# Sliding-window attention whose second half is cut by query chunk instead of by head group, with more staging buffers and earlier loads

## The chip, the cores and the metric

The kernel runs on one core of one Trainium2 chip. The metric is device time in microseconds (us) of a whole execution, the median of several runs. A separate execution, taken by the profiler, gives the rows quoted below. The engines are PE (TensorE, matmuls; PEld its weight loads), DVE (VectorE), ACT (ScalarE), POOL (GpSimd) and SP (SyncE, which issues most DMAs).

## What is computed

Two layers run on 2048 positions of width 576 and their outputs stand side by side. Layer A is attention with 32 heads of 18, where a query sees itself and the 255 positions before it; layer B is a long convolution whose filter comes from a state-space model.

```python
def A(x, wqkv, wo):                      # 32 heads, Dh = 18, window W = 256
    q, k, v = split(x @ wqkv)
    scores = q @ k.T * Dh ** -0.5
    mask = (i - j >= 0) & (i - j < W)
    p = softmax(where(mask, scores, -1e9))
    return concat_heads(p @ v) @ wo
def B(u, A, B, C, log_dt, Dskip):
    dt = exp(log_dt)
    K = real(einsum("dn,dnl,dn->dl", C, exp(dt * A * l), dt * B))
    return irfft(rfft(pad(u)) * rfft(pad(K)))[:L] + u * Dskip
return concatenate([A(...), B(...)], -1)
```

## The kernel before

**Stages.** `front` loads and scales the weights. Then the projection to q, k and v (`proj`, stored to the DRAM buffers `qd` and `vd`), the filter's tables (`tables`) and the first transform stage of the input (`s1_u`) are interleaved. Then attention begins, and everything that is left runs inside it.

**Filter's first stage.** `s1_k` has 16 parts. Each does 8 matmuls (line 521), copies the results to two staging tiles `g1` of the pool `s1k` (line 145 on ScalarE, every fourth on VectorE, line 147) and stores them to `gk` over SP (line 523). The pool has 4 buffers. Two parts run ahead of attention, seven more before the first scores, seven in items 0 to 6.

**Units and items.** Heads come in eight groups `g` of four. Attention's work is cut into 16 units: units 0 to 7 are groups 0 to 7 for queries 0 to 1023 (the first half, `hf` = 0), units 8 to 15 the same groups for queries 1024 to 2047. A unit has two chunks `c` of 512 queries, a chunk three banks `b`: 96 items. In loop step `n` of `attention` the scores of item `n` are emitted together with the values of item `n - 2`, some steps of the maxima for a later unit, and parts of the convolution and of the output projection. `merge` takes the next step of the stream that is furthest behind its share; the instructions of each engine run in the order in which they are emitted. `self.after(1, ...)` puts a DMA at the beginning of the next item.

**One unit.** `load_unit(i + 2)` is called at the first item of unit `i` and loads Q and K over SP (lines 681, 682) into one of three sets, and V over GpSimd's queue (line 685) into one of four V buffers. `gmax` copies Q into a block-diagonal form `qb` (line 693), multiplies 32 blocks of 32 queries by their 288 keys (line 702, PSUM pool `ring` of 3 banks), and VectorE takes the maximum of each with a bias mask (line 709); the result goes into a row of Q by DMA. It starts at the fourth item of the unit two before. `scores` multiplies K and Q (line 743, PSUM pool `stp`), ScalarE takes the exponential (line 745), GpSimd clears the triangles at the window's edges (line 754). `values` accumulates in PSUM (line 766); ScalarE copies out (line 774).

**Normalization.** `norm`, for units 0 to 13, moves the denominators by small DMAs over SP (line 810), spreads their reciprocals by a transpose (line 817), multiplies (825), splits into two float16 parts (826, 828) and stores them to `od` over GpSimd's queue (line 832, four DMAs). `norm_chunk`, for units 14 and 15, does it for 512 queries with two transposes on VectorE (lines 781 to 794) without SP. Group 7 is not stored: it stays in SBUF (`h7`).

**Output projection.** The output's rows are four chunks of 512, a chunk 8 pieces (4 row tiles by 2 column halves). A whole piece has 15 matmuls (line 978): three products for each of four blocks `k` of 126 rows of `od`, and three for group 7. `wo_operands` loads the blocks from `od` over SP (line 966). Chunks 0 and 1 (`wo_first`) run in items 62 to 85. Chunks 2 and 3 need the second half of all groups, so `wo_part` does k = 0, 1 of both (16 pieces of 6 matmuls, items 87 to 96, results kept in SBUF), and `wo_rest` the other 9 matmuls of each piece and the addition on VectorE (line 1012): for half of chunk 2 at item 97, for the others behind all else.

**Convolution.** `conv` starts at item 10. In its last stage (from about item 78) 16 steps each load a tile of the spectra `h` over SP (line 615) and of the input over GpSimd's queue (line 619), two steps ahead; VectorE multiplies the input by Dskip (line 633, one step ahead), PE transforms (line 637), VectorE adds into `y`, which has two buffers (line 640), and SP stores (`self.after`, line 134).

**Attention's start.** `attention_start` loads unit 0, then the identity and the bias mask (`att_consts`), then unit 1; then `gmax(0)` is merged with `s1_k`.

## Time and profile before

| | us |
|---|---|
| runs: median of 3 (lowest, highest) | 1009.77 (1008.87, 1018.71) |
| profiled execution | 1002.49 |
| its span, first to last instruction | 1000.8 |
| PE, DVE, POOL, ACT busy | 833.7, 684.2, 598.9, 560.9 |
| first scores begin | 445.8 |
| last value matmuls end | 977.3 |

A busy time is a sum over instructions; matmuls are pipelined, so a busy PE is not PE at its peak. In the answers by stretches each row has the stretch, its length, then for each engine the busy us and in brackets the number of instructions, the granted clock of TensorE as a share of its full clock, the mean share of the time that the 16 DMA engines were busy, and GB/s. In a row in order of time stand start, duration, engine, line, operation, output, input, shape, count, and in square brackets the engine's idle time before it and what ended it. In a row of groups stand busy time, mean ns, idle time before and what ended it. In a row of waits stand the total, the number of times and, for one engine's list, the longest.

### The profile page before, as it was taken

How to read it: one execution, taken by the hardware profiler on the slowest of the kernel's cores; microseconds unless marked ns; L12 is line 12 of the kernel's file. 1: busy time of each engine (PE TensorE's matmuls, PEld its weight loads, DVE VectorE, ACT ScalarE, POOL GpSimd, SP SyncE). 2: the span in 40 equal slices, each digit the busy share in tenths (PEclk: the TensorE clock that was granted, in tenths of full speed). 3: DMA queues.
4: the chain of work that ended last, by engine and by line, in shares of the span. 5: the costliest groups of instructions: out<-in, count | busy, mean ns of one | idle time of the engine just before them, and what ended most of it. 6: DMA issues, size and time to landing. Idle time of an engine off the chain costs nothing.

```text
span 1000.8 us, 26986 instructions
## 1 busy us (share of the span) xinstructions
PE 833.7 (83%) x10364; PEld 443.5 (44%) x10364; DVE 684.2 (68%) x1815; ACT 560.9 (56%) x901; POOL 598.9 (60%) x733
## 2 busy tenths in 40 slices
PE   0287989888999999689988888788888999988687
PEld 0034645464566557444433333333333444444345
DVE  5689477467574576357678778888777666668464
ACT  1455766566766775235655565565655555545460
POOL 2118567485686677602476867577866775666680
PEclk9998999999999999989899999999999999999899
DMA  8824535434543532634475675754658573687863
GB/s 304 257 71 123 141 106 123 100 83 114 129 105 76 134 94 76 220 126 148 131 161 149 172 184 166 177 151 124 145 153 202 139 182 104 168 213 232 225 175 128
DMA packets 139240, 150.35 MB, mean 150 GB/s; under 512 B 37464, under 2 KB 106248, under 8 KB 138344
## 3 DMA queue, kind: packets, MB, share of 16 engines
q1 hardware_dynamic: 131144, 131.75, 49.1%
q0 software_dynamic: 6512, 15.04, 5.6%
q10 hardware_dynamic: 1456, 1.84, 0.6%
q8 instruction: 82, 1.34, 0.6%
q14 instruction: 46, 0.38, 0.1%
HBM read 86.30 MB, written 61.01 MB: 147 GB/s over the span
## 4 chain that ended last, share of the span: by engine, by line
PE 24%; DVE 12%; issue 6%; DMA 4%; ACT 3%; POOL 3%; SPq 1%; DVEq 0%; ACTq 0%; POOLq 0%
PE po L766 5%; PE r L702 4%; PE r L978 4%; PE r L570 3%; PE r L562 3%; PE ST L743 2%; DVE jk L709 2%; ACT P L745 2%; DVE qb L693 2%; DVE osb L825 2%; DMA ol<-od 1%; POOL P L754 1%; DVE t L592 1%; DVE t L594 1%; PE r L637 1%
## 5 line engine op out<-in xcount | busy, mean ns | idle before, releaser
L709 DVE CUSTOM_DVE_ANT_0 jk<-r,bias 128x288 f32<-128x288 f32 (+7 forms) x512 | 199.8, 433 | 86.4 <-PE r L702 84.8
L754 POOL TENSOR_SCALAR_AFFINE_SELECT P<-P 128x512 f32<-128x512 f32 x240 | 168.9, 732 | 142.8 <-ACT P L745 140.2
L745 ACT ACTIVATE P<-ST,esc 128x1024 f32<-128x1024 f32 (+1 forms) x192 | 202.0, 1059 | 93.1 <-PE ST L743 92.6
L442 POOL TENSOR_TENSOR m<-A,tr 128x1024 f32<-128x1024 f32 x72 | 143.5, 2015 | 79.6 <-PE kp L480 79.5
L702 PE MATMUL r<-K,qb 128*64 128x288 f16 (+7 forms) x1024 | 130.6, 296 | 40.0 <-DVE qb L693 11.8
L702 PEld LDWEIGHTS <-qb 128*64 128x64 f16 x1024 | 58.4, 109 | 125.7 <-issue 72.9
L766 PE MATMUL po<-P,V 128*32 128x256 f32 (+2 forms) x1408 | 100.3, 397 | 11.9 <-ACT osb L774 3.9
L599 POOL TENSOR_TENSOR Y<-t,t 64x288 f32<-64x288 f32 x64 | 55.1, 861 | 63.3 <-DVE t L594 61.3
L480 PE MATMUL kp<-Q,m 128*32 128x64 f32 x4608 | 81.1, 223 | 11.3 <-issue 3.4
L480 PEld LDWEIGHTS kp<-Q,m 128*32 128x32 f32 x4608 | 70.1, 111 | 38.7 <-issue 24.4
L743 PE MATMUL ST<-Q,K 64*128 64x384 f16 (+2 forms) x704 | 73.6, 282 | 1.3 <-DMA Q<-mt 1.3
L420 POOL TENSOR_TENSOR tr<-tr,mab 128x768 f32<-128x768 f32 x18 | 33.9, 1884 | 43.6 <-ACT tr L389 43.6
L180 PE MATMUL pp<-xh,wh 128*128 128x512 f16 x180 | 51.0, 404 | 9.5 <-ACT xh L211 8.9
L766 PEld LDWEIGHTS po<-P,V 128*32 128x32 f32 x1408 | 36.2, 110 | 46.9 <-issue 28.7
L383 DVE TENSOR_TENSOR k<-x,k 128x512 f32<-128x512 f32 (+1 forms) x54 | 34.0, 641 | 33.5 <-ACT k L382 33.1
L180 PEld LDWEIGHTS <-wh 128*128 128x128 f16 x324 | 31.9, 100 | 53.8 <-issue 21.3
L600 POOL TENSOR_TENSOR Y<-t,t 64x288 f32<-64x288 f32 x64 | 52.0, 813 | 3.8
L180 PE MATMUL pp<-xh,wl 128*128 128x512 f16 x180 | 48.3, 394 | 0.0
L384 DVE TENSOR_SCALAR ab<-k 128x512 int32<-128x512 int32 (+1 forms) x54 | 47.8, 897 | 0.4
L342 DVE SCALAR_TENSOR_TENSOR qst<-pp,qst 128x512 f16<-128x512 f32 x36 | 24.7, 685 | 30.9 <-ACT qst L341 23.0
L145 ACT ACTIVATE g<-pp 128x288 f32<-128x288 f32 x75 | 29.1, 414 | 29.9 <-PE pp L521 19.1
L521 PE MATMUL pp<-ut,w 128*128 128x288 f32 x128 | 39.8, 433 | 6.6 <-DVE qst L342 5.2
(175 smaller groups left out, 1716.2 us busy)
## 6 DMA issues: line engine op xcount, KB each, us to landing
qd<-qst SPq DMA_DIRECT2D x72, 128.0 KB
gx<-g SPq DMA_DIRECT2D x32, 288.0 KB
gk<-g SPq DMA_DIRECT2D x32, 288.0 KB
tx<-gx SPq DMA_DIRECT2D x32, 288.0 KB
tk<-gk SPq DMA_DIRECT2D x32, 288.0 KB
h<-ho SPq DMA_DIRECT2D x16, 576.0 KB
Q<-qd SPq DMA_DIRECT2D x32, 216.0 KB
raw<-in_x_dram SPq DMA_DIRECT2D x16, 320.0 KB
```

What stands on the lines that cost most here:

```text
L180: self.nc.tensor.matmul(ps, u, v, start=(i == 0), stop=(i == len(ops) - 1))
L384: nc.vector.tensor_scalar(ab.bitcast(I32), k, 0x7FFFFFFF, None, op0=OP.bitwise_and)
L442: self.nc.gpsimd.tensor_tensor(m, A[:, ch, a0:a0 + 8].unsqueeze(3).to_broadcast(sh), tr[:, ch, part, 0:8].unsqueeze(2).to_broadcast(sh), o ...
L480: nc.tensor.matmul(kp[32 * st:32 * st + 32, c % 2 * JJ2 + j, :], m[:, ch, a0:a0 + 32], Q[:, ch, term % 2, :], start=(term == 0), stop=(ter ...
L599: nc.gpsimd.tensor_tensor(Y[par][0:64], t1[sl, 0], t2[sl, 0], op=OP.subtract)
L600: nc.gpsimd.tensor_tensor(Y[par][64:128], t1[sl, 1], t2[sl, 1], op=OP.add)
L702: nc.tensor.matmul(ps[64 * b:64 * b + 64, :n], self.qb[:, b, t, :], d["K"][:, b, k0:k0 + n], start=True, stop=True, skip_group_check=True)
L709: nc.vector.tensor_tensor_reduce(out=jk[:, :n], in0=ps[:, :n], in1=self.bias[:, 288 - n:], scale=1.0, scalar=-3e38, op0=OP.add, op1=OP.max ...
L743: nc.tensor.matmul(ps[:, u, o:o + n], d["K"][h, jp, k0:k0 + 128], d["Q"][h, jp, q0:q0 + n], start=True, stop=True, skip_group_check=True)
L745: nc.scalar.activation(pt[:, 2 * jp:2 * jp + 2, lo:hi], ps[:, :, lo:hi], AF.Exp, scale=self.esc)
L754: nc.gpsimd.affine_select(v, v, pattern=[[0, 4], [sg, 128]], compare_op=OP.is_ge, fill=0.0, base=-1 if far else 0, channel_multiplier=-sg)
L766: nc.tensor.matmul(self.po[32 * j:32 * j + 32, t0 * 128:t1 * 128], V[:, kb * 76 + 19 * j:kb * 76 + 19 * j + 32], pt[:, j, o:o + (t1 - t0) ...
```

## The change

Unit `i` of the second half, `i = 8 + 4c + g'`, is now groups 2g' and 2g' + 1 for the single chunk of 512 queries at 1024 + 512c. `runs(i)` gives its two runs, each with its own 768 keys, so K's tile grows from 1280 to 1536 columns and V's from 10 to 12 blocks of 76 (`key0` gives a chunk's first key block). Loads and stores of these units are two of half the queries in place of one. All groups of output chunk 2 come from units 8 to 11. Its projection is whole pieces (`wo_whole(2, 3)`) in items 84 to 96; `wo_part` does k = 0, 1 of chunk 3 alone, and `wo_rest` keeps seven PSUM banks (four of `stp`, three of `ring`) for chunk 3: k = 2 of seven pieces, k = 3, then group 7 and the addition piece by piece. Chunks 0 and 1 run in items 58 to 79. `norm` is used to unit 11 and `norm_chunk` from unit 12; unit 15's runs without pauses and stores group 6 over SP, after which block k = 3 of chunk 3 is loaded.

Besides: the pool `s1k` has 8 buffers in place of 4, and two parts of `s1_k` move from ahead of the first scores to items 7 and 8; at attention's start the order is unit 0, query copies, bias mask, identity, eight steps of `gmax(0)` with two parts of `s1_k`, unit 1, the rest; V is loaded three items after Q and K, into three buffers in place of four; the maxima's unused output `jk` is one fixed tile in place of one of a pool; and the convolution's last stage loads three steps ahead in place of two.

```diff
-HK = HQ + 256
+HK = HQ + 512
...
-        nx = [loadh(0), loadh(1)]
+        nx = [loadh(0), loadh(1), loadh(2)]
...
-            if qd < 14:
-                nx.append(loadh(qd + 2))
+            if qd < 13:
+                nx.append(loadh(qd + 3))
...
+    def runs(self, i):
+        if i < 8:
+            return [(i, 0, 0, HQ, 0, 256, HQ)]
+        c, g = divmod(i - 8, 4)
+        q0 = HQ + 512 * c
+        return [(2 * g + e, q0, 512 * e, 512, q0 - 256, 768 * e, 768) for e in range(2)]
+    def key0(self, i, c):
+        return 4 * c if i < 8 else 6 * c
...
+        for g, q0, qc, qn, k0, kc, kn in self.runs(i):
+            for u in range(2):
+                nc.sync.dma_start(d["Q"][64 * u:64 * u + 54, :, qc:qc + qn], heads(216 * g, q0, qn)[u])
+                nc.sync.dma_start(d["K"][64 * u:64 * u + 54, :, kc:kc + kn], heads(32 * 54 + 18 + 216 * g, k0, kn)[u])
+    def load_v(self, i):
+        V = self.V[i] = self.p["v"].tile([128, 12 * 76 + 16], F32, name="V")
+        for g, q0, qc, qn, k0, kc, kn in self.runs(i):
...
+            nc.gpsimd.dma_start(V[:, e - n:e].rearrange("p (t e) -> p t e", e=76),
+                                self.vd[g][:, k0 // 128:(k0 + kn) // 128])
...
-                jk = self.p["m"].tile([128, 288], F32, name="jk")
+                jk = self.jk
...
-                k0, q0 = (4 * c + r) * 128, (4 * c + t0) * 128
+                k0, q0 = (self.key0(i, c) + r) * 128, (4 * c + t0) * 128
...
+        g, q0 = self.runs(i)[c][:2]
+        for j in range(4 if g < 7 else 0):
+            f0 = 72 * g + 18 * j
+            (nc.gpsimd if i < 15 else nc.sync).dma_start(
+                self.od[:, f0:f0 + 18, q0:q0 + 512].rearrange("a p n -> p a n"), h[32 * j:32 * j + 18])
...
+                if k == 3 and i < 14:
+                    self.load_v(i + 2)
...
-            if n < 7:
+            if n < 9:
                 streams.append((part(s1k, 1), 1))
...
-            if n in (59, 67):
-                self.wo_operands((n - 59) // 8, 0, 4)
-            if 62 <= n < 86:
-                k = share(n - 62, 16, 24)
+            if n in (56, 64):
+                self.wo_operands((n - 56) // 8, 0, 4)
+            if n == 82:
+                self.wo_operands(2, 0, 4)
+            if n in (90, 96):
+                self.wo_operands(3, *((0, 2) if n == 90 else (2, 3)))
+            if 58 <= n < 80:
+                k = share(n - 58, 16, 22)
                 streams.append((part(wo0, k), k))
...
-            if n in (84, 88):
-                self.wo_operands(2 + (n - 84) // 4, 0, 2)
-            if n in (94, 96):
-                self.wo_operands(2 + (n - 94) // 2, 2, 4)
-            if 87 <= n < 97:
-                k = share(n - 87, 16, 10)
+            if 84 <= n < 97:
+                k = share(n - 84, 8, 13)
+                streams.append((part(wo2, k), k))
+            if 91 <= n < 97:
+                k = share(n - 91, 8, 6)
                 streams.append((part(wo1, k), k))
-            if n == 97:
-                streams.append((part(wo2, 4), 4))
...
-            if n >= 2 and n < 86 and (n - 2) % 6 == 5:
+            if n >= 2 and n < 74 and (n - 2) % 6 == 5:
                 norms.append(self.norm(items[n - 2][0]))
...
+        self.wo_operands(3, 3, 4)
...
-        for g in (wo1, wo2, self.wo_rest(3)):
-            for _ in g:
-                pass
+        self.wo_rest()
...
+    def wo_rest(self):
+        nc = self.nc
+        pss = []
+        for t in range(2):
+            ps = self.p["stp"].tile([128, 2, 512], F32, name="ST")
+            pss += [ps[:, 0, :288], ps[:, 1, :288]]
+        pss += [self.wo_ring() for n in range(3)]
+        for k in (2, 3):
+            for n in range(7):
+                self.wo_mm(pss[n], 3, n // 2, n % 2, k, k + 1, k == 2, False)
+        for n in range(8):
+            t, h = n // 2, n % 2
+            if n < 7:
+                ps = self.wo_mm(pss[n], 3, t, h, 4, 4, False, True)
+            else:
+                ps = self.wo_mm(self.wo_ring(), 3, t, h, 2, 4, True, True)
+            if h == 0:
+                y = self.p["wo2"].tile([128, D], F32, name="ya")
+            nc.vector.scalar_tensor_tensor(y[:, h * 288:h * 288 + 288], ps, self.osc, self.acc[n],
+                                           op0=OP.mult, op1=OP.add)
...
-            self.pool(ek, "s1k", 4, side="right")
+            self.pool(ek, "s1k", 8, side="right")
...
-            for n, b, s in (("att", 1, None), ("m", 2, None), ("v", 4, None), ("ring", 3, PSUM)):
+            for n, b, s in (("att", 1, None), ("m", 2, None), ("v", 3, None), ("ring", 3, PSUM)):
...
-                for _ in part(s1k, 1):
-                    pass
-                merge((self.gmax(0), 19), (part(s1k, 5), 5))
+                gm = self.gmax(0)
+                next(gm)
+                self.att_consts()
+                merge((part(gm, 8), 8), (part(s1k, 2), 2))
+                self.load_unit(1)
+                self.load_v(1)
+                merge((gm, 10), (part(s1k, 2), 2))
```

143 lines of the change are left out of this document (69 added, 74 removed).

## The prediction

> **What bounds the kernel now.** I read the page first, then the busy time by stretches, then who waits for whom, and last the rows in order of time at the two ends of attention.
>
> ```profile
> span 1000.8 us, 26986 instructions
> PE 833.7 (83%) x10364; PEld 443.5 (44%) x10364; DVE 684.2 (68%) x1815; ACT 560.9 (56%) x901; POOL 598.9 (60%) x733
> core 0: us, PE busy (x) PEld busy (x) DVE busy (x) ACT busy (x) POOL busy (x), PEclk, DMA share, GB/s
> 415.00:420.00 5.00, 2.38 (x15) 1.38 (x11) 1.60 (x13) 0.00 (x0) 0.99 (x3) 1.00 0.83 231
> 420.00:425.00 5.00, 0.73 (x2) 0.50 (x2) 0.00 (x0) 0.93 (x3) 0.00 (x0) 0.71 0.92 339
> 425.00:430.00 5.00, 4.92 (x22) 2.46 (x21) 3.37 (x17) 0.52 (x2) 0.00 (x0) 0.50 0.36 135
> 430.00:435.00 5.00, 4.31 (x22) 2.12 (x20) 2.46 (x12) 0.91 (x3) 0.00 (x0) 0.76 0.31 118
> 870.00:977.30 107.30, 88.34 (x854) 42.71 (x853) 69.29 (x184) 55.70 (x72) 75.86 (x128) 0.95 0.78 213
> 880.00:890.00 10.00, 6.33 (x60) 2.39 (x60) 6.28 (x21) 3.87 (x5) 5.23 (x9) 0.83 0.65 184
> 940.00:950.00 10.00, 4.51 (x20) 1.65 (x21) 3.48 (x7) 2.93 (x5) 3.23 (x7) 0.72 0.95 249
> 977.30:1000.80 23.50, 17.99 (x148) 13.86 (x144) 10.97 (x21) 1.23 (x2) 0.00 (x0) 0.96 0.34 121
> ```
>
> No engine is full for the whole span; TensorE comes nearest at 83%. Three places have slack that the change touches. At 415 to 425 us TensorE works 3.1 of 10 us and every engine is nearly still, while the DMA share is 0.83 and 0.92: attention's start waits for transfers. From 870 to 977.3 TensorE is busy 88.3 of 107.3 us, with holes at 880 to 890 (3.7 us idle) and 940 to 950 (5.5 us idle). From 977.3, the end of the last value matmuls, 23.5 us follow in which only the output projection runs.
>
> The profiled run took 1002.49 us, 1.7 us more than its span and 7.3 us below the median of the three runs, 1009.77 us. I add differences in us to the median, since nothing says where the runs differ.
>
> **Start of attention: minus 4.3 us.**
>
> ```profile
> 410.90 0.46 DVE L147 COPY g<-pp 128x288 f32<-128x288 f32 x1 [1.48 <-PE pp L521]
> 413.22 1.44 DVE L693 COPY qb<-Q 54x2048 f16<-54x2048 f16 x2
> 412.27 0.94 SPq L667 DMA_DIRECT2D bias<-in_c_bias_dram  x2
> 415.27 0.19 DVE L709 CUSTOM_DVE_ANT_0 jk<-r,bias 128x32 f32<-128x32 f32 x1
> 423.81 0.71 ACT L145 ACTIVATE g<-pp 128x288 f32<-128x288 f32 x2 [9.05 <-DMA gk<-g]
> 433.29 0.45 DVE L709 CUSTOM_DVE_ANT_0 jk<-r,bias 128x288 f32<-128x288 f32 x1
> 433.66 0.45 DVE L709 CUSTOM_DVE_ANT_0 jk<-r,bias 128x288 f32<-128x288 f32 x1
> 440.06 2.21 PE L521 MATMUL pp<-K,w 128*128 128x288 f32 x8
> 445.82 0.33 PE L743 MATMUL ST<-Q,K 64*128 64x384 f16 x1 [1.05 <-DMA Q<-mt]
> ```
>
> ScalarE waits 9.05 us for a store of the staging tile g, because the pool has 4 buffers (two parts of the filter's first stage) and unit 1's loads stand ahead of the stores. With 8 buffers four parts fit, and unit 1's loads come after the fourth: this wait goes. What is late next is the bias, whose clearing on VectorE and load on SP now stand behind the query copies. These follow the second part's copy, which ends at 411.36, and take 1.44 us: 412.8. Two issues (0.94 us) and a landing (from 413.21 to 415.27 at most, 2.06 us) put the first maximum at about 416, 0.7 us later than now. Behind the bias on SP stand the stores of parts 3 and 4; the eight buffers cover them. VectorE needs 0.37 us per maximum (433.29 to 433.66); with the exchange with TensorE I estimate half as much again, 1.1 us per pair, and 17.6 us for 16 pairs. Of seven parts that still run before the first scores two are done by 412.8; four of the rest, at 2.21 us and partly under VectorE, add 7 us. That ends near 438, against 445.82 for the first scores: 7.8 us. The two parts moved to items 7 and 8 (4.4 us of TensorE) come back at 0.8 of their length, 3.5 us; where the factor comes from is said below. Bounds: 0 if the bias or unit 1's late loads take the whole gain, 8 if the moved parts are hidden.
>
> The clock went to 0.50 and 0.76 in the ten microseconds after the hole, so 2.5 + 1.2 = 3.7 us of clock are lost there, which the 7.8 us hold. The Trainium skill (TensorE: Matmul & The Clock Gate, part 1 on the warmup) puts the way back to full clock at about 3.4 us of steady work at half rate, a loss of 1.7 us; as an estimate by that page the start would gain 2 us less. The trace shows the longer penalty, and I keep it.
>
> **Projection moved into attention: plus 7.2 us.**
>
> ```profile
> 741.35 0.59 ACT L774 ACTIVATE osb<-po 128x512 f32<-128x512 f32 x1
> 773.54 0.59 ACT L774 ACTIVATE osb<-po 128x512 f32<-128x512 f32 x1
> 812.34 0.59 ACT L774 ACTIVATE osb<-po 128x512 f32<-128x512 f32 x1
> 977.33 4.54 PE r L978 x36
> 986.66 10.13 PE r L978 x81
> ```
>
> A projection matmul costs 10.13 / 81 = 0.125 us. Chunk 2 now has its 8 pieces of 15 matmuls in items 84 to 96 (15.0 us) and loses 8 partial pieces of 6 (6.0 us): 9.0 us more TensorE work before the last values. How much of it shows? The copies at 741.35, 773.54 and 812.34 end units 8, 9 and 10, six items apart: 32.2 us without projection, then 38.8 us with 4 pieces (60 matmuls, 7.5 us). So 6.6 of 7.5 us showed there, 0.88; the last third has more holes than that stretch, and I take 0.8. 9.0 x 0.8 = 7.2 us. Starting chunks 0 and 1 four items earlier only moves work inside the same stretch. Bounds: 1 us (all in holes) and 9.
>
> **Prefetch of three instead of two: minus 8 us.**
>
> ```profile
> DVE X L633 <- DMA X<-in_u_dram: 9.6, 3, 4.2
> DVE t L633 <- DMA t<-in_u_dram: 8.3, 3, 4.3
> DVE t L640 <- DMA out_dram<-t: 5.6, 3, 2.0
> PE r L637 <- DMA tx<-h: 4.7, 1, 4.7
> ```
>
> In the convolution's last stage VectorE, working in order, stands 17.9 us for the input rows, TensorE 4.7 us for the spectra; gmax and scores stand behind. Requests now go out one item earlier, which is 5 to 6 us. The buffers allow it: the set taken belongs to the step before, whose output store precedes the load on SP anyway, so SP gets no new wait. Chunk 2's operands are now asked for whole at item 82, two items behind the stores they wait for, as the halves were; the loads and output stores queued behind them on SP are what the third step of prefetch covers. The output rows keep two buffers, so L640's 5.6 us can stay. TensorE's two holes are 3.7 + 5.5 = 9.2 us; I take 8 of them. Bounds: 0 (the DMA share of 0.78 is the limit, not the order) and 11 (with the clock lost at 0.83 and 0.72).
>
> **Other work in the second half: plus 2.5 us.**
>
> ```profile
> L832 POOL DMA_DIRECT2D od<-oh x52 | 31.8, 614 | 0.0
> L685 POOL DMA_DIRECT2D V<-vd x16 | 9.4, 589 | 0.1
> L817 DVE STREAM_TRANSPOSE spread<-dent 128x1024 f32<-128x1024 f32 x14 | 17.4, 1245 | 0.5
> 982.33 0.70 DVE L781 STREAM_TRANSPOSE rb<-osb 128x512 f32<-128x512 f32 x1
> 984.10 0.69 DVE L791 TENSOR_TENSOR osb<-osb,rb 128x512 f32<-128x512 f32 x1
> PE po L766 <- POOL P L754: 3.5, 6, 0.8
> od<-oh POOLq DMA_DIRECT2D x52, 72.0 KB, 2.9
> od<-oh POOLq DMA_DIRECT2D x8, 36.0 KB, 2.9
> ```
>
> GpSimd issues 20 more stores (12 in units 8 to 10, 8 in units 12 and 13) at 0.614 us and 8 more V loads at 0.589 us: 17 us over eight units. Behind them in its queue stand the triangle masks that the values wait for; TensorE waited 3.5 us for these between 500 and 980 us, and I add 1.0. Units 12 and 13 take the per-chunk normalization: 982.33 to 984.10 is 1.77 us of VectorE per chunk, 3.5 per unit, for 1.25 plus two small operations; some 3 us more for both, half showing, 1.5. SP loses 8 small transfers by it. Four more Q and K issues per unit and K's 1.2 times the columns lie three items ahead of their use, and V, asked for three items later, still eleven: 0. K's clearing grows by a fifth, ahead of the first copies: 0. The single jk is written by VectorE alone, in order: 0, and no gain. Bounds for the part: 0 and 25 (the second is a rival).
>
> **Tail: minus 9 us.**
>
> ```profile
> 977.39 0.60 ACT L774 ACTIVATE osb<-po 128x512 f32<-128x512 f32 x1 [0.53 <-PE po L766]
> 985.48 0.69 DVE L794 TENSOR_TENSOR h<-osb,h 128x512 f16<-128x512 f32 x1 [0.69 <-ACT h L792]
> 996.81 0.52 DVE L1012 SCALAR_TENSOR_TENSOR ya<-r,osc,Y 128x288 f32<-128x288 f32 x1 [0.59 <-PE r L978]
> ```
>
> Before, 16 pieces of 9 matmuls (18 us) and the last normalization share the 23.5 us, and VectorE reaches the normalization only at 982.33, behind chunk 2's additions. Now ScalarE's copy ends 0.7 us after the last values and the normalization needs 985.48 + 0.69 - 982.33 = 3.8 us: operands at 4.6. Meanwhile TensorE does 42 matmuls of seven pieces, 5.3 us. Then VectorE's eight additions set the pace, 8 x 0.55 after 0.4: about 10.1 us. From the last addition's end (997.33) to the span's end is 3.5 us. That makes 13.6. Group 6 of chunk 3 is ready only three items before the end; its store and load, each near the 2.9 us of a store, can put the k=3 matmuls back by 0 to 2.5 us, and I take 1.0: 14.6, against 23.5, a gain of 9 (bounds 7 and 10).
>
> **Sum.** -4.3 + 7.2 - 8 + 2.5 - 9 = -11.6 us; the profiled run would come to 990.9, and 1009.77 - 11.6 = 998.2, said as 998. By its own bounds this case reaches from 990 to 1004.
>
> **Rivals.** First, the moved matmuls lie wholly in holes. From item 87 on there are no maxima to find and transfers set the pace (share 0.95 at 940 to 950), so chunk 2's pieces cost 1 us instead of 7.2, and the start gives 2 us more: -11.6 - 6.2 - 2 = -19.8, 990. For it speaks that TensorE has 19 idle us in the last 107; against it 6.6 of 7.5 us.
>
> Second, the prefetch gives nothing: the holes are those of full transfer queues, whose bytes don't shrink. Then 8 us are missing: 1006. For it speaks the 0.78 to 0.95 share, against it that 17.9 us of waiting is on loads sent one step ahead.
>
> Third, slower: GpSimd becomes the bound in units 8 to 15. Its 17 us of issues delay masks, and the input rows' loads, which it issues too, come late again so the prefetch's 8 us are lost: -11.6 + 17 - 1 + 8 = +12.4, 1022. It decides once GpSimd's share in those units, 75.9 of 107.3 us now, nears its whole time; 17 us over eight units bring it to three quarters only.
>
> Fourth, halved transfers. If each unit's split load landed one store's 2.9 us later and gmax waited for it, eight units would pay 23 us: 1009.77 - 11.6 + 23 = 1021. The two sizes of od land in 2.9 us alike, so halving saves no latency, but the loads have three items of lead. The Trainium skill (DMA: Bandwidth & Descriptors, Bandwidth) asks for large batches of a MiB or more and speaks against splitting; the equal 2.9 us agree with a fixed part.
>
> That the projection isn't in fact inside attention is no rival: chunk 2 needs units 8 to 11 only, done by item 73.
>
> **Chances.** Forecast 0.48, first rival 0.22, second 0.16, third 0.12, fourth 0.02. About 1% (10.1 us) is what a measurement of this kernel can tell from no change. The forecast's case is above that gain in 0.30 and below in 0.18; so faster 0.30 + 0.22 = 0.52, same 0.18 + 0.16 = 0.34, slower 0.14. The range leaves out the slower rivals and what lies under 985: 985 to 1011.
>
> **What would show it.** In the new profile: no wait of ScalarE for gk before the first scores, and these near 438 us; VectorE's waits at the input rows under 8 us in all; TensorE over 90% busy in the last 100 us before the last values; 14 to 15 us from there to the end; GpSimd below 80% in units 8 to 15. A span between last values and end over 18 us, or TensorE holes of 5 us in the last third, would make the prediction wrong.

## The result and the profile after

| | before | after |
|---|---|---|
| median of the runs, us | 1010.28 | 1064.08 |
| profiled execution, us | 1002.49 | 1065.24 |
| its span, us | 1000.8 | 1062.9 |
| first scores begin, us | 445.8 | 443.4 |
| last value matmuls end, us | 977.3 | 1042.6 |

The changed kernel is slower: 1.0533 of the time before, 95% interval 1.0497 to 1.0569, some 54 us. The prediction was 998 us. The profiled execution of the kernel before is 7.8 us below its median and that of the changed kernel 1.2 us above its own, so the two spans differ by 62 us.

The page of the changed kernel answers to the lines shown of before. Its first two lines are the span and the busy times, the third is VectorE's group of maxima (busy time, mean ns, idle time before and what ended most of it).

```profile
span 1062.9 us, 27120 instructions
PE 861.7 (81%) x10364; PEld 450.6 (42%) x10364; DVE 707.7 (67%) x1813; ACT 561.1 (53%) x901; POOL 614.5 (58%) x769
...
L724 DVE CUSTOM_DVE_ANT_0 jk<-r,bias 128x288 f32<-128x288 f32 (+7 forms) x512 | 222.9, 435 | 125.0 <-PE r L717 74.5
```

TensorE has the same 10364 matmuls and is busy 28 us longer, at a mean granted clock of 0.960 against 0.977. The same group of maxima in the kernel before is this:

```profile
L709 DVE CUSTOM_DVE_ANT_0 jk<-r,bias 128x288 f32<-128x288 f32 (+7 forms) x512 | 199.8, 433 | 86.4 <-PE r L702 84.8
```

One maximum takes as long as before, 435 ns against 433, yet the group's busy time is 23 us greater. Busy time is the time that the engine's line is covered, so instructions that overlapped before overlap less now.

To see where the time came from, I divided both profiles at ScalarE's copies of the finished values (osb from po, L774 before, L789 after; each ends one chunk of a unit; the item is the loop step `n` in which the copy stands). The first stretch begins at the last copy of the filter's K tile (L486), since everything ahead of it is unchanged. The last three columns are experiments that are told below.

| from copy to copy, by item | before | after | two jk tiles | and V later, block earlier | and operands earlier |
|---|---|---|---|---|---|
| K copy to 13 | 107.3 | 120.5 | 100.8 | 103.9 | 100.7 |
| 13 to 46 | 178.0 | 186.6 | 180.0 | 180.1 | 180.1 |
| 46 to 58 | 65.2 | 70.7 | 72.0 | 67.3 | 65.8 |
| 58 to 73 | 93.5 | 103.5 | 100.5 | 99.5 | 99.5 |
| 73 to 79 | 30.3 | 43.3 | 41.6 | 39.3 | 38.1 |
| 79 to 85 | 40.5 | 45.7 | 43.9 | 41.8 | 37.9 |
| 85 to 97 | 56.8 | 62.6 | 59.6 | 58.7 | 60.0 |
| 97 to the end | 23.4 | 20.3 | 20.3 | 16.6 | 15.7 |

The loss is spread over the whole of attention. It begins in the first stretch and in items 13 to 46, where the units are still grouped as before and no projection has begun. Whatever the regrouping costs, another cause works there too. A stretch can differ by 2 or 3 us without any change in it: the prefetch alone, a kernel told below, has the code of before up to about item 78, and its first four stretches are 110.5, 180.1, 65.2 and 94.0 us.

### The profile page after: what moved, and what is told of

Same layout as the page of the kernel before. It is cut to its first block, busy times and chain, and to the rows that moved or that the text cites. A ratio compares the mean times of both kernels' runs of the same rounds, so it can differ in the third digit from the quotient of the medians.

```text
span 1062.9 us, 27120 instructions
## 1 busy us (share of the span) xinstructions
PE 861.7 (81%) x10364; PEld 450.6 (42%) x10364; DVE 707.7 (67%) x1813; ACT 561.1 (53%) x901; POOL 614.5 (58%) x769
## 4 chain that ended last, share of the span: by engine, by line
PE 44%; DVE 23%; issue 10%; DMA 9%; ACT 6%; POOL 5%; SPq 2%; DVEq 0%; ACTq 0%; POOLq 0%
PE pp L180 8%; DVE jk L724 6%; PE r L717 5%; PE po L781 4%; PE r L1005 4%; PE kp L480 4%; PE ST L758 3%; PE r L570 3%; PE r L562 3%; PE pp L521 3%; PE r L521 2%; PE x L372 2%; DMA ol<-od 2%; DMA c_ct<-in_c_ct_dram 2%; DVE qb L707 1%
## 5 line engine op out<-in xcount | busy, mean ns | idle before, releaser
L724 DVE CUSTOM_DVE_ANT_0 jk<-r,bias 128x288 f32<-128x288 f32 (+7 forms) x512 | 222.9, 435 | 125.0 <-PE r L717 74.5
L769 POOL TENSOR_SCALAR_AFFINE_SELECT P<-P 128x512 f32<-128x512 f32 x240 | 166.7, 723 | 168.3 <-ACT P L760 165.9
L717 PE MATMUL r<-K,qb 128*64 128x288 f16 (+7 forms) x1024 | 139.1, 300 | 67.7 <-DVE m L724 21.9
L781 PE MATMUL po<-P,V 128*32 128x256 f32 (+2 forms) x1408 | 105.2, 412 | 14.2 <-POOL P L769 7.9
L599 POOL TENSOR_TENSOR Y<-t,t 64x288 f32<-64x288 f32 x64 | 52.8, 824 | 76.9 <-DVE t L594 75.0
L480 PEld LDWEIGHTS kp<-Q,m 128*32 128x32 f32 x4608 | 69.3, 110 | 43.0 <-issue 23.4
L781 PEld LDWEIGHTS po<-P,V 128*32 128x32 f32 x1408 | 36.7, 113 | 51.5 <-issue 30.7
L180 PE MATMUL pp<-xh,wh 128*128 128x512 f16 x180 | 48.5, 388 | 9.4 <-ACT xh L211 8.9
L600 POOL TENSOR_TENSOR Y<-t,t 64x288 f32<-64x288 f32 x64 | 51.9, 811 | 3.8
L562 PE MATMUL r<-tk,w 128*64 128x288 f32 x256 | 42.3, 433 | 6.4 <-DVE m L724 6.2
L562 PE MATMUL r<-tx,w 128*64 128x288 f32 x256 | 40.5, 423 | 7.9 <-DVE m L724 5.4
```

Of the source, the lines that this page charges most:

```text
L180: self.nc.tensor.matmul(ps, u, v, start=(i == 0), stop=(i == len(ops) - 1))
L480: nc.tensor.matmul(kp[32 * st:32 * st + 32, c % 2 * JJ2 + j, :], m[:, ch, a0:a0 + 32], Q[:, ch, term % 2, :], start=(term == 0), stop=(ter ...
L562: nc.tensor.matmul(ps[64 * par:64 * par + 64], w2[:, par, 64 * part:64 * part + 64], t[:, par, 2 * hs:2 * hs + 2, :], start=True, stop=True)
L599: nc.gpsimd.tensor_tensor(Y[par][0:64], t1[sl, 0], t2[sl, 0], op=OP.subtract)
L717: nc.tensor.matmul(ps[64 * b:64 * b + 64, :n], self.qb[:, b, t, :], d["K"][:, b, k0:k0 + n], start=True, stop=True, skip_group_check=True)
L724: nc.vector.tensor_tensor_reduce(out=jk[:, :n], in0=ps[:, :n], in1=self.bias[:, 288 - n:], scale=1.0, scalar=-3e38, op0=OP.add, op1=OP.max ...
```

## The experiments

### The unused output alone

The maxima write an output `jk` that nobody reads. In order of time on VectorE, the changed kernel's maxima look like this (start, duration, line, operation):

```profile
428.45 0.46 DVE L724 CUSTOM_DVE_ANT_0 jk<-r,bias 128x288 f32<-128x288 f32 x1
428.84 0.08 DVE L724 DVE_READ_ACCUMULATOR2_ANT m<- 128x1 f32 x1
429.06 0.46 DVE L724 CUSTOM_DVE_ANT_0 jk<-r,bias 128x288 f32<-128x288 f32 x1
429.45 0.08 DVE L724 DVE_READ_ACCUMULATOR2_ANT m<- 128x1 f32 x1
429.67 0.46 DVE L724 CUSTOM_DVE_ANT_0 jk<-r,bias 128x288 f32<-128x288 f32 x1
```

They start 0.61 us apart; in the kernel before it was 0.37 us (433.29 and 433.66 in the prediction's rows). Each instruction takes 0.45 us either way, so before, the next one started while the last was still running. As I read it, with one tile each maximum writes where the last one writes, and the program makes it wait for the last one's completion; with two tiles in turn it waits for the one before that, which is done long since. The profile has no row for such a wait, so what can be tested is the number of tiles. For this, one kernel took the single tile into the kernel before, and one gave the changed kernel two tiles again. The second has them in bf16, for want of space; the values are not used. Type and place differ between the two tests, the number of tiles is what they share.

```diff
 (b_jk1, from the kernel before)
+        self.jk = ap.tile([128, 288], F32, name="jk")
...
-                jk = self.p["m"].tile([128, 288], F32, name="jk")
+                jk = self.jk
 (a_jk2, from the changed kernel)
-        self.jk = ap.tile([128, 288], F32, name="jk")
...
-                jk = self.jk
+                jk = self.p["m"].tile([128, 288], BF, name="jk")
```

> The kernel before with one fixed tile jk for the maxima's unused output and nothing else changed. Theory 1 (one tile makes each maximum wait for the end of the one before, start to start 0.61 us where it was 0.37): VectorE's maxima stand 0.61 us apart in a row of maxima, and the time rises by 25 to 45 us, to 1035 to 1055. Theory 2 (the regrouped units and the transfers of the last third are what costs): within 5 us of 1010.

> The changed kernel with jk as two tiles again (of half the bytes, bfloat16, for lack of space; its values are used by nothing). Theory 1: maxima 0.37 to 0.39 us apart again, 1010 to 1035. Theory 2: above 1055.

The single tile in the kernel before: 1047.38 us, a ratio of 1.0381 (1.0335 to 1.0427), 38 us more. Two tiles in the changed kernel: 1029.59 us, 1.0214 (1.0157 to 1.0271), 34 us less than the change as a whole (32 us by the ratios). VectorE's rows of the first:

```profile
658.70 0.46 DVE L710 CUSTOM_DVE_ANT_0 jk<-r,bias 128x288 f32<-128x288 f32 x1 [0.17 <-PE r L703]
659.31 0.46 DVE L710 CUSTOM_DVE_ANT_0 jk<-r,bias 128x288 f32<-128x288 f32 x1
659.92 0.46 DVE L710 CUSTOM_DVE_ANT_0 jk<-r,bias 128x288 f32<-128x288 f32 x1
660.53 0.46 DVE L710 CUSTOM_DVE_ANT_0 jk<-r,bias 128x288 f32<-128x288 f32 x1
```

and those of the second:

```profile
713.24 0.45 DVE L723 CUSTOM_DVE_ANT_0 jk<-r,bias 128x288 bf16<-128x288 f32 x1
713.62 0.45 DVE L723 CUSTOM_DVE_ANT_0 jk<-r,bias 128x288 bf16<-128x288 f32 x1
```

The distance follows the number of tiles: 0.61 us with one, 0.38 us with two. 512 maxima at 0.24 us more would be 123 us; 38 us of it show, since many maxima wait for TensorE anyway (84.8 us in the row above). This is the greater part of the loss: 32 to 38 of 54 us. Some 20 us are left.

### The regrouping alone, and the prefetch alone

The first kernel has two jk tiles and the regrouping, but loads two steps ahead, four staging buffers and the start of before. The second is the kernel before with loads three steps ahead.

```diff
 (a_units, from a_jk2)
-        nx = [loadh(0), loadh(1), loadh(2)]
+        nx = [loadh(0), loadh(1)]
...
-            if qd < 13:
-                nx.append(loadh(qd + 3))
+            if qd < 14:
+                nx.append(loadh(qd + 2))
...
-            self.pool(ek, "s1k", 8, side="right")
+            self.pool(ek, "s1k", 4, side="right")
...
-            if n < 9:
+            if n < 7:
 (b_pf3, from the kernel before)
-        nx = [loadh(0), loadh(1)]
+        nx = [loadh(0), loadh(1), loadh(2)]
...
-            if qd < 14:
-                nx.append(loadh(qd + 2))
+            if qd < 13:
+                nx.append(loadh(qd + 3))
```

> The regrouped units with their projection alone: two jk tiles, loads two steps ahead, four staging tiles and the old order at attention's start. Theory 1 (regrouping itself does what I predicted of it, plus 9.7 us in attention and minus 9 in the tail): 1000 to 1015. Theory 2 (regrouping costs in the last third): 1025 to 1045.

> The kernel before with loads three steps ahead in the convolution's last stage and nothing else changed. As predicted: minus 8 us, 1002. Rival (the transfer queues are full there, or the earlier loads stand in front of others): 1008 to 1020, with VectorE's waits for the input rows gone and its waits for the output tiles longer.

The regrouping alone, with its loads at the places that the change gave them, took 1036.7 us, 1.0279 (1.0229 to 1.0329): it costs 27 us. The prefetch alone took 1012.22 us, 1.0012 (0.9982 to 1.0042): no change that can be measured. VectorE's waits in that kernel (total, times, longest) say why:

```profile
DVE t L640 <- DMA out_dram<-t: 22.8, 7, 6.3
```

The 17.9 us at the input rows (L633) are gone from the list, and the wait for the output rows' store (L640), 5.6 us before, has grown to 22.8 us. The loads come earlier, the step gets through its first half sooner, and then it wants its output tile while that tile's store is still on its way. The sum of both, 23.5 us before, is 22.8 now.

### V's load behind the stores

In the changed kernel V is asked for at the fourth item of a unit. In order of time on GpSimd of the kernel with two jk tiles, around 870 us:

```profile
865.94 1.81 POOL L768 TENSOR_SCALAR_AFFINE_SELECT P<-P 128x512 f32<-128x512 f32 x3 [4.61 <-ACT P L759]
867.70 4.97 POOL L854 DMA_DIRECT2D od<-oh  x8
872.71 0.58 POOL L698 DMA_DIRECT2D V<-vd  x1
...
873.33 0.56 POOL L698 DMA_DIRECT2D V<-vd  x1
873.90 1.82 POOL L768 TENSOR_SCALAR_AFFINE_SELECT P<-P 128x512 f32<-128x512 f32 x3
875.67 2.00 POOL L619 DMA_DIRECT2D X<-in_u_dram  x4
877.66 1.96 POOL L619 DMA_DIRECT2D t<-in_u_dram  x4
...
882.70 0.50 POOL L619 DMA_DIRECT2D X<-in_u_dram  x1 [3.09 <-DMA X<-in_u_dram]
...
885.69 2.98 POOL L768 TENSOR_SCALAR_AFFINE_SELECT P<-P 128x512 f32<-128x512 f32 x5
```

Eight stores, two V loads, three triangle masks (L768) and the input rows' loads stand in one queue. The masks at 873.90 come 1.2 us later for the two V loads and their clearings. Between them and the next masks at 885.69 lie 10 us of the input rows' loads, and at 882.70 GpSimd itself stands 3.1 us for an earlier one of these (4.1 us with the two short stands behind it). On TensorE the value matmuls wait for the mask:

```profile
886.39 1.94 PE L780 MATMUL po<-P,V 128*32 128x256 f32 x16 [5.95 <-POOL P L768]
```

and the stretches around it show what follows (length, busy time of PE, PEld, DVE, ACT and POOL with the number of instructions, granted clock, DMA share, GB/s):

```profile
860.00:882.00 22.00, 19.13 (x189) 10.01 (x188) 14.73 (x56) 12.62 (x18) 15.00 (x28) 1.00 0.54 138
882.00:888.00 6.00, 1.61 (x16) 0.55 (x16) 0.42 (x4) 1.33 (x2) 4.29 (x8) 0.65 0.99 239
888.00:892.00 4.00, 4.00 (x27) 2.15 (x23) 0.29 (x1) 0.50 (x1) 0.67 (x2) 0.67 0.76 212
```

The clock is 0.65 in the hole and still 0.67 in the four full microseconds behind it, so the stall is paid longer than it lasts. One kernel moved V's load two items on, away from the stores; another moved the stores of units 8 to 14 to SP as well, to see whether GpSimd's load as such matters.

```diff
 (a_v5, from a_jk2)
-                if k == 3 and i < 14:
+                if k == 5 and i < 14:
 (a_v5_od, from a_v5; norm's stores likewise from unit 8)
-            (nc.gpsimd if i < 15 else nc.sync).dma_start(
+            nc.sync.dma_start(
```

> The changed kernel with two jk tiles, and V loaded at a unit's sixth item in place of its fourth. Theory 1 (GpSimd's queue: at the fourth item the V issues stand right behind the od stores, 3.8 to 6.1 us in a row, the masks behind them come late, TensorE stands 1.8 to 6 us and its clock halves): items 46 to 58 go back from 71.9 to 65 to 67 us, items 73 to 79 from 41.6 to 36 to 39, the whole 1018 to 1024 against 1029.6. Theory 2 (the transfers of the regrouped units, not GpSimd's issues): both stretches stay, within 3 us of 1029.

> As the run before, and the od stores of units 8 to 14 go over SP in place of GpSimd's queue. Theory 1: GpSimd's stand still before its loads of input rows (3 us at item 77) goes too, and items 73 to 85 fall from 85.5 to 70 to 78 us; the whole 1008 to 1018. Theory 2 (SP's queue, in order, waits for VectorE's products and holds back loads): items 73 to 85 no shorter, the whole 1020 or more.

V two items later: 1020.81 us, 1.0113 (1.0069 to 1.0156), 9 us less than with V at the fourth item; the two intervals just miss each other. GpSimd's rows at the same place:

```profile
865.72 4.96 POOL L854 DMA_DIRECT2D od<-oh  x8
870.70 1.81 POOL L768 TENSOR_SCALAR_AFFINE_SELECT P<-P 128x512 f32<-128x512 f32 x3
872.46 2.04 POOL L619 DMA_DIRECT2D X<-in_u_dram  x4
874.49 1.96 POOL L619 DMA_DIRECT2D t<-in_u_dram  x4
```

The masks now come right behind the stores. The input rows' loads begin 6.7 us after the first store where it was 8.0, GpSimd stands 0.9 us for earlier loads where it was 4.1, and TensorE waits 2.15 us for the masks where it was 5.95. The V loads themselves are 1.2 us of this; why the stand shrank by 3 us more these rows don't show. Around 690 us, before any input rows are loaded, the effect is plain. TensorE's wait with V at the fourth item and at the sixth:

```profile
688.71 0.42 PE L780 MATMUL po<-P,V 128*32 128x128 f32 x8 [1.80 <-POOL P L768]
```

```profile
692.89 0.43 PE L780 MATMUL po<-P,V 128*32 128x128 f32 x8 [0.60 <-POOL P L768]
```

The difference, 1.2 us, is what the two V loads and their clearings take on GpSimd. The stretch from item 46 to 58 went from 72.0 to 65.9 us and that from 73 to 79 from 41.6 to 35.6 us, and TensorE's waits at po for P fell from 13.1 to 4.1 us between 500 and 985 us. Part of the 72.0 us is the clock. Behind the wait of 1.80 us it was 0.62 for eight microseconds; in the kernel with the earlier block (next section), whose V is at the fourth item too and whose wait there is also 1.80 us, it stayed at 1.00, and that stretch took 67.6 us:

```profile
690.00:698.00 8.00, 7.70 (x44) 2.75 (x44) 3.01 (x11) 1.94 (x3) 1.84 (x4) 0.62 0.24 69
```

```profile
694.00:702.00 8.00, 7.44 (x66) 3.15 (x59) 5.06 (x17) 3.29 (x5) 4.26 (x6) 1.00 0.30 92
```

The gain in time is seen a second time: with the earlier block in both kernels, moving V took the ratio from 1.0183 (1.014 to 1.0227) to 1.0092 (1.0057 to 1.0126).

The stores on SP brought nothing more: 1026.25 us, 1.0162 (1.0122 to 1.0202). TensorE's waits for the masks fell from 4.1 to 3.5 us only. So the order on GpSimd cost time at a few places, and its load as such does not show; what the stores cost in SP's queue instead is not separated.

### The end and the start

In the changed kernel block k = 2 of chunk 3's operands is asked for at item 96. Its place in SP's queue, in order of time:

```profile
1039.72 1.39 SPq L815 DMA_DIRECT2D od<-oh  x4
...
1041.75 0.32 SPq L994 DMA_DIRECT2D oh<-od  x1
1042.12 0.41 SPq L994 DMA_DIRECT2D ol<-od  x1
1042.82 0.31 SPq L994 DMA_DIRECT2D oh<-od  x1
1043.18 0.39 SPq L994 DMA_DIRECT2D ol<-od  x1
```

```profile
1042.60:1062.90 20.30, 11.32 (x72) 7.57 (x72) 6.92 (x13) 1.23 (x2) 0.00 (x0) 0.90 0.33 117
```

Four stores, which wait for a normalization, stand ahead of block k = 2 (1041.75 and 1042.12), so that it leaves SP just before the last values end (1042.6 us); the last two rows are block k = 3. TensorE then stands 1.3 and 0.9 us for block k = 2, its clock is 0.57 from 1045 to 1049 us and 0.90 over the whole 20.3 us. One kernel asks for the block one item earlier. Another takes the new start of attention, alone, into the kernel before: eight staging buffers, the new order and two parts of `s1_k` in items 7 and 8.

```diff
 (a_tail, from a_jk2)
-            if n in (90, 96):
+            if n in (90, 95):
 (b_start, from the kernel before; the bias is set ahead of the identity; pool, items and attention_start as in the change)
-                for _ in part(s1k, 1):
-                    pass
-                merge((self.gmax(0), 19), (part(s1k, 5), 5))
+                gm = self.gmax(0)
+                next(gm)
+                self.att_consts()
+                merge((part(gm, 8), 8), (part(s1k, 2), 2))
+                self.load_unit(1)
+                merge((gm, 10), (part(s1k, 2), 2))
```

> The changed kernel with two jk tiles, and block k = 2 of chunk 3 asked for at item 95 in place of 96, so ahead of unit 15's od stores in SP's queue. Theory 1 (the tail is long because this load stands behind stores that wait for the last normalization, and the clock has halved by then): from the last values to the end 15 to 17 us in place of 19.7, the whole 2 to 4 us less than 1029.6. Theory 2 (block k = 3 or the additions set the tail): 19 to 20 us as before.

> The kernel before with the new start of attention alone: 8 staging tiles, the new order, two parts moved to items 7 and 8. As predicted: minus 4.3 us, with ScalarE's 9 us wait gone and first scores 8 us earlier counted from the clearing of the first set. Rival (the bias comes later and eats it): within 2 us of before.

The earlier block: 1027.43 us, 1.0183 (1.014 to 1.0227), 2 us less than with two jk tiles alone and inside its interval, but the end itself is plain: 16.7 us behind the last values where it was 20.3. The first row is block k = 2 in SP's queue, 6.9 us ahead of the last values; TensorE's waits for it are gone, and its clock stays at 1.00 while there are matmuls.

```profile
998.19 0.33 SPq L993 DMA_DIRECT2D oh<-od  x1
...
1005.10:1021.80 16.70, 9.49 (x72) 6.71 (x70) 6.93 (x13) 1.20 (x2) 0.00 (x0) 0.94 0.35 125
```

The new start: 1004.06 us, 0.9949 (0.9917 to 0.998), a gain of 6 us. Its rows on ScalarE, VectorE and TensorE (three answers of one view):

```profile
412.97 1.04 ACT L486 ACTIVATE K<-kp 128x512 f32<-128x512 f32 x1 [6.11 <-PE kp L480]
...
423.41 0.19 DVE L709 CUSTOM_DVE_ANT_0 jk<-r,bias 128x32 f32<-128x32 f32 x1 [3.02 <-DMA bias<-in_c_bias_dram]
...
444.08 0.33 PE L743 MATMUL ST<-Q,K 64*128 64x384 f16 x1 [0.88 <-DMA Q<-mt]
```

From the K tile's last copy to the first scores it takes 31.1 us; before it was 40.2 us (405.64 to 445.82). The wait of 9.05 us for the staging tile is gone. VectorE now stands 3.0 us for the bias, and the first maximum comes 10.4 us after the K tile's last copy where it was 9.6. To item 13 there are 104.2 us against 107.3: two thirds of the 9 us come back with the two moved parts. That stretch took 110.5 and 108.6 us in two other kernels told here with the old start, and 104.0 in another with the new one, so the gain there is 3 to 6 us.

### Prefetch of two, projection behind attention, a third output tile

Three more kernels asked what the other parts are worth in the company they have in the changed kernel. Two rest on the changed kernel with two jk tiles, V at the sixth item and the earlier block, the third on the kernel before with loads three steps ahead.

```diff
 (a_pf2, from a_jk2 with V and block moved)
-        nx = [loadh(0), loadh(1), loadh(2)]
+        nx = [loadh(0), loadh(1)]
...
-            if qd < 13:
-                nx.append(loadh(qd + 3))
+            if qd < 14:
+                nx.append(loadh(qd + 2))
 (a_wo2out, from a_jk2 with V and block moved)
-            if 84 <= n < 97:
-                k = share(n - 84, 8, 13)
-                streams.append((part(wo2, k), k))
 (b_pf3_y3, from b_pf3; the pool fy3 has one buffer)
-            y = fy.tile([128, D], F32, name="t2")
+            y = fy.tile([128, D], F32, name="t2") if qd % 3 else self.p["fy3"].tile([128, D], F32, name="t3")
```

> The changed kernel with two jk tiles, V at the sixth item, block k = 2 ahead of unit 15's stores (by the runs before, these three should make about 1017), and loads two steps ahead. Theory 1 (the wait only changes its place, from the input rows to the output tiles, whichever the depth): 1014 to 1021, VectorE's waits for the input rows 10 us or more again and those for the output tiles under 6. Theory 2 (the earlier loads crowd the last third): 1010 or less.

> The same kernel (loads three steps ahead) with chunk 2's eight pieces behind attention instead of in items 84 to 96; 15 us of TensorE work leave that stretch. Theory 1 (inside attention they cost 0.8 of their length): items 85 to 97 about 12 us shorter than 62, the way from the last values to the end about 15 longer, the whole 1018 to 1022. Theory 2 (they lie in holes there): the stretch under 5 us shorter, the whole 1026 or more. Theory 3 (they cost more there than their length, by disturbing the order): the whole under 1014.

> The kernel before with loads three steps ahead and a third buffer for the output tile y. Theory 1 (with three steps ahead the wait went from the input rows to the two output tiles): the waits of L640 fall from 22.8 us to under 10 and the time to 1000 to 1006. Theory 2 (the transfers' throughput is the limit, whatever the buffers): waits of the same sum in some place, the time within 3 us of 1011.

Loads two steps ahead: 1022.48 us, 1.0116 (1.0061 to 1.0171), where the same kernel with three has 1.0092 (1.0057 to 1.0126; it is run below): the two can't be told apart. VectorE's waits are the mirror of those above:

```profile
DVE X L633 <- DMA X<-in_u_dram: 13.3, 5, 4.1
DVE t L633 <- DMA t<-in_u_dram: 9.7, 5, 3.1
...
DVE t L640 <- DMA out_dram<-t: 2.8, 3, 1.3
```

23.0 us at the inputs and 2.8 at the output with two, 15.4 us at the output and nothing at the inputs with three. A third output tile took that wait down from 22.8 to 13.7 us in the kernel before, and the time was 1008.99 us, 0.9973 (0.9943 to 1.0003): still none that can be told from no change.

Chunk 2's eight pieces behind attention: 1026.38 us, 1.0158 (1.0103 to 1.0213). From item 73 to 97 this needs 129.1 us, and 139.8 us with the pieces inside; behind the last values it needs 31.0 us against 16.6. So 15 us of matmuls (120 at 0.125 us) cost 10.7 us inside attention, 0.71 of their length, and 14.4 us behind it. Inside is the better place, by about 4 us in these profiles and 7 us by the ratios (1.0158 and 1.0092), whose intervals overlap.

### Chunk 2's operands

One stretch was still unexplained: from item 79 to 85 the regrouped kernel needs more time although 45 projection matmuls have left it. In that stretch chunk 2's operands are asked for whole, at item 82. SP's queue in the kernel with V and block moved (a_v5_tail):

```profile
913.17 0.96 SPq L993 DMA_DIRECT2D oh<-od  x1
914.19 0.47 SPq L993 DMA_DIRECT2D ol<-od  x1
...
916.86 5.49 SPq L134 DMA_DIRECT2D out_dram<-t  x4
```

The convolution's four output stores behind the load need 5.49 us to issue, where other groups of four need 1.8 to 2.8, and VectorE then stands for its output tile. Two kernels moved this load alone: half of it to item 74, or all of it to item 86 with the pieces in items 88 to 96.

```diff
 (a_op_early, from a_v5_tail)
-            if n == 82:
-                self.wo_operands(2, 0, 4)
+            if n in (74, 82):
+                self.wo_operands(2, *((0, 2) if n == 74 else (2, 4)))
 (a_op_late, from a_v5_tail)
-            if n == 82:
+            if n == 86:
...
-            if 84 <= n < 97:
-                k = share(n - 84, 8, 13)
+            if 88 <= n < 97:
+                k = share(n - 88, 8, 9)
```

> The changed kernel with two unused outputs, V's load at the sixth item, and chunk 3's block k = 2 asked for at item 95: the base for the next two. If the gains seen one by one add up (8.8 us for V, 2.2 us for the block), 1018 us, a ratio of 1.009; if they overlap, 1021 us. Between the copies of items 79 and 85 it should need 46 us, with 11 us of VectorE's waits for the convolution's output tile in them.

> The base with half of chunk 2's operands (blocks 0 and 1) asked for at item 74 and the other half at item 82. Theory 1, the whole operand load holds up the output stores behind it: 0.5 MB less at that place at some 235 GB/s is 2.2 us less ahead of the store, so VectorE's waits there fall from 11 to 5 us or less, the stretch from 46 to 41 to 43 us, the time by 3 to 5 us. Theory 2, the regrouped loads and GpSimd's work make the stretch longer: within 1.5 us of the base, the waits at the output tile as before.

> The base with chunk 2's operands asked for at item 86, when the convolution's last rows are nearly through, and its eight pieces in items 88 to 96. Theory 1: the stretch between the copies of items 79 and 85 falls from 46 us to 39 to 41 us (one piece of 2 us leaves it as well), the waits at the output tile to under 4 us; the stretch from 85 to 97 grows by 1 to 4 us for the piece and the shorter time for it; the time falls by 2 to 5 us. Theory 2: the first stretch loses the piece's 2 us alone, and the time is within 1.5 us of the base.

The base took 1017.89 us, 1.0092 (1.0057 to 1.0126). Half the operands earlier: 1014.03 us, 1.006 (1.0029 to 1.009); all of them later: 1019.03 us, 1.0106 (1.0056 to 1.0156). The stretch from 79 to 85 was 41.8 us in the base (not 46, as expected: the hole lies partly in the stretch before), 37.9 with the early half and 36.7 with the late load. VectorE's waits in the stretch are, of the base and of the kernel with the early half:

```profile
DVE t L640 <- DMA out_dram<-t: 6.9, 2, 5.2
```

```profile
DVE t L640 <- DMA out_dram<-t: 2.9, 1, 2.9
```

So the load does hold up the output stores, for some 4 us of that stretch (in the late kernel a piece of 2 us has left it as well). The late kernel gives them back in the next one (63.0 us against 58.7), where eight pieces now share nine items. That the early one keeps its 4 us in the time is likely but not sure, as its interval overlaps the base's and its profiled execution, 1006.54 us, is the fastest of its ten.

### A version faster than both

Of the parts tried alone in the kernel before, only the start gains. One kernel joined it with loads three steps ahead and the third output tile, all in the kernel before.

```diff
 (b_best, from b_start; the pool fy3 has one buffer)
-        nx = [loadh(0), loadh(1)]
+        nx = [loadh(0), loadh(1), loadh(2)]
...
-            if qd < 14:
-                nx.append(loadh(qd + 2))
+            if qd < 13:
+                nx.append(loadh(qd + 3))
...
-            y = fy.tile([128, D], F32, name="t2")
+            y = fy.tile([128, D], F32, name="t2") if qd % 3 else self.p["fy3"].tile([128, D], F32, name="t3")
```

> The kernel before with the new start of attention, loads three steps ahead and a third output tile: the parts that gained or might. Theory 1: 994 to 1001. Theory 2 of the run before: 1002 to 1006, the start's gain alone.

It took 1003.01 us, 0.9928 (0.99 to 0.9957): faster than both kernels, by less than 1%, and hardly more than the start alone.

## Why the prediction was wrong

**The single jk, put at 0.** This is the step that failed: "The single jk is written by VectorE alone, in order: 0, and no gain." Order on one engine was taken to mean that nothing waits. The runs show 38 us when it is done alone and 34 us when it is undone. Half of the evidence was in the rows I quoted: instructions of 0.45 us starting 0.37 us apart overlap. That they no longer do with one tile, 0.61 us apart, is what the runs added. None of my rivals had it. The prediction with 38 us in this place would have been 1036 us.

**Prefetch, minus 8 us.** The rows of waits were right, the 17.9 us at the inputs did go, and the time didn't follow (1.0012 alone; 1.0116 and 1.0092 in the regrouped kernel). The prediction let L640's 5.6 us stay as they were; they took over the whole wait. The second rival named this outcome, 1006 us, with full queues for its cause.

**Other work of the second half, plus 2.5 us.** V "asked for three items later" was priced by its lead, eleven items, and put at 0; what cost was its place in GpSimd's queue, behind four or eight stores and ahead of the masks: 9 us. I priced the issues (17 us) but let them fall evenly, 1.0 us for the masks. The third rival had the mechanism, GpSimd's issues delaying masks, and the wrong form: no run showed its total to matter (moving the stores off it gained nothing), while the order at a few places did.

**Projection moved into attention, plus 7.2 us.** The price was right in the profiles: 0.71 of the matmuls' length against my 0.8, so 6.4 instead of 7.2 us for 9.0. Two things beside it were not. The whole load of chunk 2's operands was said to be covered by the third step of prefetch; it held up output stores and cost 4 us in its stretch. And starting chunks 0 and 1 four items earlier was put at 0, as moved inside the same stretch. In the kernel of the table's last column the stretches from item 58 to 79 need 137.6 us with the early operands and 123.8 before, those from 79 to 97 about the same as before (97.9 and 97.3). The row of the kernel before for items 73 to 79 shows what the work was moved into:

```profile
849.70:880.00 30.30, 28.29 (x286) 14.68 (x284) 21.69 (x80) 18.36 (x25) 20.70 (x35) 1.00 0.69 167
```

TensorE was busy 28.3 of 30.3 us there, and little room was left for more. From item 58 to 79 the records count 240 projection matmuls in the changed order and 180 before: 60 more, 7.5 us, came out of a stretch in which transfers set the pace (DMA share 0.82) and went into fuller ones. From item 58 to 73 there are 165 where there were 120; TensorE's time in them is 22.1 us where it was 16.1, and the stretch takes 99.5 us where it took 93.5. So these 45 matmuls match the whole loss of that stretch, 6 us. From 73 to 79 there are only 15 more (1.9 us) for 7.8 us, and the rest of that is not theirs by this count. No run moved these two chunks alone, so their share of the 14 us stays unproven.

**Tail, minus 9 us.** The 14.6 us from the last values to the end were 20.3, a gain of 3 us. The 0 to 2.5 us that I allowed for group 6 were of the right kind and too small: it was not the store's and load's own time but the queue. With block k = 2 one item earlier 16.7 us are left, and 15.7 with the operands earlier too, so the layout of the tail did bring 7 to 8 us. Some 2 us are still missing: VectorE's additions stand 2.4 us for the stores of their output tiles, a wait that the sum didn't have.

**Start, minus 4.3 us.** Right in the mechanism, and in the size within the noise: minus 6 us by the runs (2 to 8 by the interval), 3.1 us in the profile. ScalarE's wait went, and the first maximum came 0.8 us later, where 0.7 was expected. Of the time to the first scores 9.1 us came off, where 7.8 was expected. But the 7.8 doesn't follow from its parts: 416, 17.6 and 7 add up to 440.6 and not to 438, a gain of 5.2, so that its nearness to 9.1 is in part luck.

Among the prediction's own signs two came as said, no wait at the input rows and none of ScalarE for the stores to gk. Two failed: TensorE was busy 79.7 of the last 100 us before the last values, where over 90% was said, and the tail took over 18 us.

Put together by ratios: 1.0533 with everything, 1.0214 with two jk tiles, 1.0092 with V's load and the block moved, 1.006 with the operands earlier too. About two thirds of the loss is one tile that has nothing to do with the regrouping, and most of the rest is the place of three loads in their queues. Without these the regrouping does not gain either: what is left holds the start's gain, 6 us, so the rest of the change still costs some 12 us. The projection's early start, with the 6 us from item 58 to 73, is the likeliest part of it; it was not tried alone.

## What to carry to other kernels

An output that nobody reads still has an address: give back-to-back instructions of one engine two tiles in turn, and look in the trace whether their starts lie closer together than they are long before you take one away. When a load is moved, price its place in the queue of the engine that issues it, with what stands between it and the next instruction that somebody waits for. A wait that a prefetch removes is a gain only if the same step's other end, here its output tile, is free in time.

## What the runs showed of the hardware that I had not expected

VectorE starts a maximum of 0.45 us 0.37 us after the last one when their outputs are two tiles in turn, and 0.61 us after it when both write one tile. The difference, 0.24 us, is over half the instruction's length; I read it as a wait for the last one's completion. The Trainium skill (VectorE: DVE Perf Modes, on the drain you can't avoid) reports that eight copies took 13.88 us with a semaphore behind each or only behind the last, so that the semaphore costs nothing extra there. The trace here differs, on another instruction: for these maxima on 288 columns the one tile costs 0.24 us each, and 38 us in the kernel.

Of GpSimd, a store or load issued takes 0.5 to 0.6 us in its order (eight stores in 4.97 us), and behind the eighth load of the input rows it stood 3.1 us, until an earlier one had landed (882.70 us in the rows above); masks queued behind that wait with it.

TensorE's clock did not follow every short stall alike. Behind two waits of the same 1.80 us at the same place of two kernels it was 0.62 for eight microseconds in one and 1.00 in the other.
